# Loading q and k of the first four chunks uncast on SyncE's queue and transposing them in fp32

## The chip, the core and the metric

The kernel runs on one core of one Trainium2 chip. TensorE (PE in the profile; PEld is its weight load) multiplies matrices, VectorE (DVE), ScalarE (ACT) and GpSimd (POOL) work elementwise, SyncE (SP) only issues DMAs. The metric is the device time of one execution in microseconds, the median over runs.

## The reference

The first half is a decaying linear attention with q, k, v of shape (4, 8, 768, 64), that is batch 4, 8 heads, 768 positions, 64 channels; the second half a feed-forward block over the 3072 tokens of 512 channels that come out.

```
for b in range(nb):                       # blocks of 64 positions
    intra = (qb @ kb^T * Dmask) @ vb      # Dmask[i,j] = lam**(i-j) for i >= j, else 0
    inter = (qb * lam**(pos+1)) @ kv_state
    out[block] = intra + inter
    kv_state = lam**64 * kv_state + (kb * lam**(63-pos))^T @ vb
x = out as (batch*positions, heads*channels)
h = x @ w_in                              # 512 -> 2048
g = where(h > 0, h, exp(min(h, 0)) - 1)
return g @ w_out                          # 2048 -> 512, fp32
```

All inputs and the output are fp32. The kernel multiplies in fp16 and sums in fp32.

## The kernel before

The kernel uses blocks of 128 positions. A chunk is one block of one batch with all 8 heads, 128 x 512; there are 24, numbered so that chunks 0 to 3 are the first blocks of the four batches. Chunks 0 to 3 are handled one at a time, later ones in pairs. Each chunk goes through these steps, and the letters are those of the order strings:

- loads of q, k and v. GpSimd issues them (`emit_load`, L109); its DMAs cast fp32 to fp16 on the way. Only q0 comes another way: it is loaded as fp32 on SyncE's queue (L117) and cast by VectorE (L127).
- T: q and k are transposed, 4 + 4 transposes of 128 x 128 (L283). VectorE scales q on the way out of PSUM (L290), ScalarE copies k (L291). From chunk 8 on, DMA transposes on SyncE's queue do this (L268).
- S: scores, 8 matmuls in pairs (L302); VectorE multiplies them by the mask (`pp`, L318).
- P: `pp` times v (L338), plus the state times q from chunk 4 on (L344); ScalarE or VectorE evacuates the result as `xt`, the input of the feed-forward part.
- d, U, M: GpSimd scales k (`kd`, L174), TensorE multiplies it with v (L397, L406), VectorE adds it to the state (L416, L418), GpSimd decays the old state first (`stt`, L378). z and Z set the two copies of a batch's state to zero.
- `1:g:j`: a quarter of the first feed-forward matmul of chunk g, 16 matmuls into `psH` (L478). It uses pieces 2j and 2j+1 of w_in (`i0` to `i7`). ScalarE makes exp and relu of it (L484, L485), VectorE combines them to `g` (L457). `psH` has two buffers.
- `2:g:j`: a quarter of the second, 4 matmuls of 512 columns into `psM` (L499), with pieces 2j and 2j+1 of w_out (`o0` to `o7`).
- `wN`: N dummy matmuls on zeros (L84); ten more stand at the start.

The order is written out by hand: `OPEN` is TensorE's order of steps from the start up to about chunk 8, after which a rule goes on. Each engine works through its instructions in that order and waits in place. `POOL_ORDER` is GpSimd's own order: loads of chunks (k0, q1, ...), weight pieces (i, o), kd (d) and state decays (m). At most eight of GpSimd's DMAs are under way: the ninth issue waits for the landing of the first. `FIRST` orders the preparation: `c0` is the table of scales qs (ScalarE), `c1` the mask (VectorE), `c2` the scales for kd. `BANKS` gives each step its PSUM banks.

The deferred work of VectorE and ScalarE on results (pp, xt, state updates) goes into a list `late`, of which each `1:` and `2:` step takes one entry; a U step empties it.

Of the kernel before, what the change touches and what calls it, by code (L numbers as in the profile page):

```python
# [662 lines left out]
```

## Time and profile before

| | us |
|---|---|
| median of 3 runs | 216.19 (215.58 to 216.25) |
| the profiled execution, whole | 215.0 |
| its span | 213.2 |
| TensorE busy | 202.7 |
| VectorE busy | 130.1 |
| ScalarE busy | 129.0 |
| GpSimd busy, DMA issues included | 96.2 |
| GpSimd's DMA queue | 79760 packets, 13.50 MB written |
| SyncE's DMA queue | 22192 packets, 10.76 MB |

In the lines of the profile a group reads: start, busy time, engine, line of the kernel, operation, output<-inputs, shape and count; in brackets the idle time of that engine just before and what ended it. Times of a group of matmuls include the latency of the last one, so groups overlap: 16 matmuls of 128 columns take 0.89 us of TensorE's time from start to start, 4 of 512 columns 0.86 us. The GB/s of a window are bytes written; a casting load reads twice what it writes.

### The profile page before, as it was taken

The numbers are of one execution on the slowest core, as the hardware profiler recorded it, in microseconds if no ns is written. First come the engines' busy times: TensorE is split into PE (matmuls) and PEld (weight loads), VectorE is DVE, ScalarE is ACT, GpSimd is POOL, SyncE is SP. The second block draws the span as 40 slices with busy tenths as digits, with TensorE's granted clock in tenths as the row PEclk, the third lists the DMA queues.
The fourth block names the chain that finished last, engine by engine and source line by source line (L and its number), as shares of the span: only waits on it lengthen the run. The fifth ranks groups of instructions, "written<-read, shape, count | busy, mean of one in ns | idle before, by whom it ended". The sixth has DMA issues, their size and how long they took to land.

```text
span 213.2 us, 5156 instructions
## 1 busy us (share of the span) xinstructions
PE 202.7 (95%) x2066; PEld 138.1 (65%) x2066; DVE 130.1 (61%) x224; ACT 129.0 (61%) x245; POOL 96.2 (45%) x115
## 2 busy tenths in 40 slices
PE   7667999999999999999999999999999999999994
PEld 2355676767686776766766766766766666666652
DVE  3936453777846888677667667667667547533321
ACT  4545654884867756676476476476476576477640
POOL 7996991999972908667166259300000000000000
PEclk9999999999999999999999999999999999999999
DMA  8999999999996999999939919999124110110112
GB/s 90 141 175 193 192 148 173 147 165 147 153 165 145 111 197 107 144 122 116 129 106 125 167 59 103 144 180 161 52 65 83 52 49 0 54 51 16 36 49 98
DMA packets 101976, 24.59 MB, mean 115 GB/s; under 512 B 92608, under 2 KB 99008, under 8 KB 101952
## 3 DMA queue, kind: packets, MB, share of 16 engines
q0 software_dynamic: 79760, 13.50, 83.1%
q1 hardware_dynamic: 22192, 10.76, 24.6%
q8 instruction: 16, 0.26, 0.5%
q14 instruction: 8, 0.07, 0.1%
HBM read 27.27 MB, written 6.29 MB: 157 GB/s over the span
## 4 chain that ended last, share of the span: by engine, by line
PE 82%; POOL 8%; DMA 7%; issue 1%; ACT 1%; DVE 0%; POOLq 0%; ACTq 0%
PE psM L499 36%; PE psH L478 35%; DMA wi<-in_moe_w_in_dram 4%; DMA wo<-in_moe_w_out_dram 3%; PE psO L338 3%; PE psS L302 3%; PE psO L344 2%; POOL kd L174 1%; POOL wi L148 1%; POOL kn L109 1%; POOL vn L109 1%; PE psU L406 1%; PE psT L283 1%; POOL qn L109 1%; POOL wo L155 1%
## 5 line engine op out<-in xcount | busy, mean ns | idle before, releaser
L478 PE MATMUL psH<-xt,wi 128*128 128x256 f16 (+1 forms) x896 | 99.3, 258 | 2.0 <-DMA wi<-in_moe_w_in_dram 1.1
L457 DVE SCALAR_TENSOR_TENSOR g<-e,psH 128x512 f16<-128x512 f32 x96 | 65.8, 686 | 56.7 <-ACT psH L485 56.0
L484 ACT ACTIVATE e<-psH 128x512 f32<-128x512 f32 x96 | 57.3, 597 | 65.0 <-PE psH L478 62.8
L499 PE MATMUL psM<-wo,g 128*128 128x512 f16 (+1 forms) x384 | 95.6, 377 | 0.7 <-DMA wo<-in_moe_w_out_dram 0.7
L478 PEld LDWEIGHTS <-wi 128*128 128x128 f16 x896 | 76.9, 98 | 27.4 <-DMA wi<-in_moe_w_in_dram 1.8
L485 ACT ACTIVATE psH<-psH 128x512 f32<-128x512 f32 x96 | 57.0, 593 | 0.0
L499 PEld LDWEIGHTS <-g 128*128 128x128 f16 x384 | 35.9, 98 | 29.3 <-issue 1.3
L318 DVE TENSOR_TENSOR pp<-psS,mask 128x512 f16<-128x512 f32 x48 | 30.8, 684 | 4.4 <-PE psS L302 4.4
L174 POOL TENSOR_TENSOR kd<-kn,ks 128x512 f16<-128x512 f16 x20 | 20.7, 1040 | 21.3 <-DMA kn<-in_k_dram 20.4
L378 POOL TENSOR_TENSOR stt<-st,upp 64x256 f32<-64x256 f16 x32 | 19.5, 608 | 14.7 <-DVE st L418 8.9
L109 POOL DMA_DIRECT2D vn<-in_v_dram x14 | 15.5, 1108 | 1.7 <-DMA wi<-in_moe_w_in_dram 1.7
L109 POOL DMA_DIRECT2D kn<-in_k_dram x14 | 15.5, 1105 | 0.8 <-POOLq L647 0.8
L525 ACT COPY osb<-psM 128x512 f32<-128x512 f32 x23 | 13.5, 590 | 3.2 <-PE psM L499 3.2
L109 POOL DMA_DIRECT2D qn<-in_q_dram x13 | 14.8, 1138 | 0.0
L418 DVE TENSOR_TENSOR st<-stt,psU 64x256 f16<-64x256 f32 x32 | 13.3, 416 | 1.2 <-PE psU L406 0.5
L361 DVE TENSOR_TENSOR xt<-psO,qs 128x512 f16<-128x512 f32 x16 | 11.0, 688 | 3.5 <-PE psO L344 3.5
L338 PE MATMUL psO<-pp,vn 128*64 128x128 f16 x192 | 12.0, 222 | 1.2 <-DMA vn<-in_v_dram 1.0
L338 PEld LDWEIGHTS <-vn 128*64 128x64 f16 x192 | 9.7, 110 | 4.6 <-issue 2.9
L344 PE MATMUL psO<-qT,st 128*64 128x128 f16 x160 | 10.0, 219 | 0.0
L344 PEld LDWEIGHTS <-st 128*64 128x64 f16 x160 | 8.9, 110 | 0.0
L302 PE MATMUL psS<-qT,kT 64*128 64x128 f16 x192 | 7.9, 218 | 0.3 <-ACT kT L291 0.3
L359 ACT CAST xt<-psO 128x512 f16<-128x512 f32 x8 | 4.4, 588 | 6.4 <-PE psO L338 4.3
(44 smaller groups left out, 72.3 us busy)
## 6 DMA issues: line engine op xcount, KB each, us to landing
out_dram<-osb SPq DMA_DIRECT2D x23, 256.0 KB, 2.2
kn<-in_k_dram POOLq DMA_DIRECT2D x10, 256.0 KB, 7.8
qn<-in_q_dram POOLq DMA_DIRECT2D x10, 256.0 KB, 6.8
vn<-in_v_dram POOLq DMA_DIRECT2D x10, 256.0 KB, 7.6
wi<-in_moe_w_in_dram POOLq DMA_DIRECT2D x8, 256.0 KB, 6.9
wo<-in_moe_w_out_dram POOLq DMA_DIRECT2D x8, 256.0 KB, 7.7
kn<-in_k_dram POOLq DMA_DIRECT2D x4, 128.0 KB, 4.2
vn<-in_v_dram POOLq DMA_DIRECT2D x4, 128.0 KB, 5.5
```

The lines of the kernel that those rows point to most:

```text
L109: nc.gpsimd.dma_start(out=t[:].rearrange("p b h d -> p (b h) d"), in_=src)
L174: nc.gpsimd.tensor_tensor(out=kd[:], in0=of(kg, g), in1=ks[:].unsqueeze(2).broadcast_to([128, H, 64]), op=ALU.mult,)
L302: nc.tensor.matmul(psS[g][hh][:, hp, :], lhsT=kt[r, hp, :], rhs=qt[r, hp, :], start=True, stop=True,)
L318: nc.vector.tensor_tensor(out=P[:], in0=pts[hh][:], in1=mask[:, hh::2, :], op=ALU.mult)
L338: nc.tensor.matmul(po[r, hp, :], lhsT=vt[:, 2 * hp + hh, :], rhs=Pt[(g, hh)][:, hp, :], start=True, stop=(cb == 0), skip_group_check=True,)
L344: nc.tensor.matmul(po[r, hp, :], lhsT=st[b][cb % 2][:, hp, r], rhs=qt[:, hp, :], start=False, stop=True, skip_group_check=True,)
L378: nc.gpsimd.tensor_tensor(out=tmp[r], in0=old[r, :, r], in1=upp[r].unsqueeze(2).broadcast_to([64, NHP, 64]), op=ALU.mult,)
L457: nc.vector.scalar_tensor_tensor(out=g[:].rearrange("p f c t -> p (f c t)"), in0=e[:], scalar=-1.0, in1=r[:], op0=ALU.add, op1=ALU.min,)
L478: nc.tensor.matmul(pH[:, f * n * 128 : (f + 1) * n * 128], lhsT=wi16[i][:, kk, w * 128 : (w + 1) * 128], rhs=xg[g0][:, kk, :], start=(kk = ...
L484: nc.scalar.activation(e[:], pH[:], AF.Exp)
L485: nc.scalar.activation(pH[:], pH[:], AF.Relu)
L499: nc.tensor.matmul(psM[g][:, cols], lhsT=gts[(g, j * FB + f)], rhs=wo16[i][:, w, cols], start=first and f == 0, stop=end and f == FB - 1, ...
```

## The change

q and k of chunks 0 to 3 are loaded as fp32 on SyncE's queue (`load_raw`). The fp32 tiles of q have two buffers, so q0, k0, q1, k1 are issued at once and q2, k2 after T0, q3, k3 after T1. T0 to T3 transpose the fp32 tiles with an fp32 identity into fp32 PSUM tiles (T3 gets a second bank); kd of these chunks reads the fp32 k. The cast of q0 is gone. GpSimd's order begins with the iota, then loads only v and weights until chunk 4. The mask is made in two halves. The zeroing of the state covers only the parts off the diagonal, in two instructions for each copy. `OPEN` up to the step `B:P4:P5:U4:U5` is in a new order; U no longer empties the list `late`, and a token `f` takes one entry of it.

```diff
--- before.py
+++ after.py
@@ -45,25 +45,27 @@
     WI = [2] * 8
     WO = [2] * 8
     POOL_ORDER = (
-        "k0 k1 iota q1 k2 v1 i0 v0 q2 i1 v2 i2 o0 i3 d0 q3 o1 i4 k3 i5 o2 o3 v3 d1 m4 d2 d3 i7 "
-        "o4 o5 i6 o7 k4 o6 q4 m5 k6 v4 q6 k10 q10 d5 d4 d6 m6 v6 k8 q8 v8 d7 m7 v10"
+        "iota v0 v1 i0 i1 v2 i2 i3 o0 o1 d0 i4 i5 o2 o3 d1 v3 d2 i7 o4 o5 i6 m4 o7 k4 o6 q4  "
+        "m5 d3 k6 v4 q6 k10 q10 d5 d4 d6 m6 v6 k8 q8 v8 d7 m7 v10"
     )
-    RAW = "q0"
-    FIRST = "q0:0 c0 c1 c2"
+    RAWBUFS = 2
+    RAW = "q0 k0 q1 k1 q2 k2 q3 k3"
+    FIRST = "c0 c2"
     OPEN = (
-        "z1 z0 z3 Z1 Z2 Z0 z2 T0 w2 T1 S0 S1 w6 P0 P1 T2 1:0:0 S2 1:1:0 P2 U0 M 1:2:0 1:0:1 2:0:0 "
-        "1:1:1 2:1:0 1:2:1 T3 2:2:0 1:0:2 S3 1:2:2 2:2:1 2:1:1 P3 1:1:2 1:3:0 2:0:1 2:0:2 "
-        "2:1:2 1:1:3 U1 1:2:3 M Z3 2:2:2 1:3:2 U2 1:3:1 2:1:3 1:0:3 T5 T4 2:2:3 1:3:3 S4:5 "
-        "2:0:3 2:3:2 2:3:0 M U3 M B:P4:P5:U4:U5 W8 2:3:3 1:4:1 T6 W9 1:4:0 T7 2:3:1 1:4:3 S6:7 "
-        "1:4:2 2:4:0 2:5:0 1:4:5 1:4:4 2:4:1 B:P6:P7:U6:U7 1:4:7 1:6:1 2:5:2 2:5:1 1:6:0 1:4:6 "
-        "2:4:2 S8:9 1:6:2 1:6:3 2:4:3 2:5:3 W11 W10 1:6:4 B:P8:P9:U8:U9 1:6:5 1:6:6 2:6:0 "
-        "2:6:1 L12 1:6:7 2:6:2 1:8:0 S10:11 2:6:3 1:8:1 2:7:0 1:8:2 2:7:1"
+        "c1 c3 Z1 Z2 Z0 T0 w1 T1 S0 S1 w3 P0 P1 z0 z1 z2 z3 w2 1:0:0 T2 1:1:0 S2 U0 1:0:1 U1 P2  "
+        "1:1:1 M f 1:2:0 f 2:0:0 f 1:2:1 2:1:0 T3 1:0:2 S3 2:2:0 1:1:2 M P3 1:2:2 2:0:1 2:1:1  "
+        "1:3:0 U2 2:2:1 2:0:2 M 1:3:1 2:1:2 1:0:3 1:1:3 Z3 2:2:2 1:2:3 1:3:2 2:1:3 T5 T4  "
+        "2:2:3 1:3:3 S4:5 2:0:3 2:3:2 2:3:0 U3 M f f f f B:P4:P5:U4:U5 W8 2:3:3 1:4:1 T6 W9  "
+        "1:4:0 T7 2:3:1 1:4:3 S6:7 1:4:2 2:4:0 2:5:0 1:4:5 1:4:4 2:4:1 B:P6:P7:U6:U7 1:4:7  "
+        "1:6:1 2:5:2 2:5:1 1:6:0 1:4:6 2:4:2 S8:9 1:6:2 1:6:3 2:4:3 2:5:3 W11 W10 1:6:4  "
+        "B:P8:P9:U8:U9 1:6:5 1:6:6 2:6:0 2:6:1 L12 1:6:7 2:6:2 1:8:0 S10:11 2:6:3 1:8:1 2:7:0  "
+        "1:8:2 2:7:1"
     )
...
     BANKS = (
         "S0=M0,M1 S1=C,D S2=D,M1 S3=D,B P0=M1 P1=B P2=B P3=D U0=M0 U1=D U2=A U3=M1 T0=M1,C "
-        "T1=D,A T2=A,D T3=D T4=M0 T5=A T6=M1 T7=D M2=C M3=M0"
+        "T1=D,A T2=A,D T3=D,C T4=M0 T5=A T6=M1 T7=D M2=C M3=M0"
     )
...
@@ -109,24 +111,16 @@
         nc.gpsimd.dma_start(out=t[:].rearrange("p b h d -> p (b h) d"), in_=src)
 
 
-    raw = {}
-    for w in RAW.split():
-        x = {"q": q, "k": k}[w[0]]
-        g0 = int(w[1:])
-        raw[w] = asb.tile([128, H, 64], FP32, name=f"raw_{w}", tag=f"raw_{w}")
-        (nc.sync if w[0] == "q" else nc.scalar).dma_start(
-            out=raw[w][:], in_=x[g0, :, 0:L].rearrange("h p d -> p h d")
-        )
+    def load_raw(w):
+        x, g0 = {"q": q, "k": k}[w[0]], int(w[1:])
+        t = asb.tile([128, 1, H, 64], FP32, name=f"raw_{w}", tag=f"raw_{w[0]}", bufs=RAWBUFS if w[0] == "q" else 4)
+        (qg if w[0] == "q" else kg)[g0] = t
+        nc.sync.dma_start(out=t[:, 0], in_=x[g0, :, 0:L].rearrange("h p d -> p h d"))
+
+    raws = RAW.split()
+    for w in raws[: 2 * RAWBUFS]:
+        load_raw(w)
     nc.scalar.preload_act_table_set("natural_log_exp_and_others")
-
-    def cast_raw(g, w, eng):
-        n = f"{w}{g}"
-        t = asb.tile([128, 1, H, 64], FP16, tag=f"{w}n1", name=f"{w}n{g}", bufs=4)
-        (qg if w == "q" else kg)[g] = t
-        if eng == 0:
-            nc.vector.tensor_copy(t[:, 0], raw[n][:])
-        else:
-            nc.scalar.copy(t[:, 0], raw[n][:])
 
     def of(tiles, g):
         g0, i = group_of[g]
@@ -190,14 +184,24 @@
 
     def emit_pool_run():
         while pool_list and pool_list[0][0] != "m":
+            if pool_list[0][0] == "d" and group_of[int(pool_list[0][1:])][0] not in kg:
+                break
             emit_pool()
 
     assert "iota" in POOL_ORDER.split("d0")[0]
     while pool_list and pool_list[0][0] not in "dm":
         emit_pool()
 
+    def zero_off(b, i, eng):
+        for hh in range(2):
+            part = st[b][i][hh * 64 : (hh + 1) * 64, :, (1 - hh) * 64 : (2 - hh) * 64]
+            if eng is nc.vector:
+                eng.memset(part, 0.0)
+            else:
+                eng.memzero(part)
+
     def zero_st1(b):
-        nc.vector.memset(st[b][1][:], 0.0)
+        zero_off(b, 1, nc.vector)
 
 
     loglam = cpool.tile([128, H], FP32, name="loglam")
@@ -205,6 +209,7 @@
     pos = cpool.tile([128, 3], FP32, name="pos")
     row = cpool.tile([128, 128], FP32, name="row")
     ident16 = cpool.tile([128, 128], FP16, name="ident16")
+    ident32 = cpool.tile([128, 128], FP32, name="ident32")
     causT = cpool.tile([128, 128], FP32, name="causT")
     loglam_p = cpool.tile([128, NHP], FP32, name="loglam_p")
 
@@ -218,7 +223,7 @@
     nc.vector.tensor_scalar_mul(pos[:, 1:2], iota_c[:], -1.0)
     nc.scalar.activation(dn[:], loglam[:], AF.Exp, scale=pos[:, 1:2])
     nc.vector.tensor_scalar(
-        out=ident16[:], in0=row[:], scalar1=pos[:, 0:1], scalar2=None, op0=ALU.is_equal
+        out=ident32[:], in0=row[:], scalar1=pos[:, 0:1], scalar2=None, op0=ALU.is_equal
     )
     nc.vector.tensor_scalar(
         out=causT[:], in0=row[:], scalar1=pos[:, 0:1], scalar2=None, op0=ALU.is_ge
...
@@ -234,11 +240,11 @@
                 qs[:, hp, :], row[:], AF.Exp, scale=loglam_p[:, hp : hp + 1]
             )
 
-    def emit_mask():
+    def emit_mask(hh):
         nc.vector.tensor_tensor(
-            out=mask[:],
-            in0=causT[:].unsqueeze(1).broadcast_to([128, H, 128]),
-            in1=dn[:].unsqueeze(2).broadcast_to([128, H, 128]),
+            out=mask[:, hh::2],
+            in0=causT[:].unsqueeze(1).broadcast_to([128, NHP, 128]),
+            in1=dn[:, hh::2].unsqueeze(2).broadcast_to([128, NHP, 128]),
             op=ALU.mult,
         )
 
@@ -273,16 +279,21 @@
 
     def att_T_pe(g):
         n = len(TAGS[f"T{g}"].split())
+        dt, ident = (FP32, ident32) if g < B else (FP16, ident16)
         pts = [
-            bank(f"T{g}", i, [128, 2 // n, NHP, 128], FP16, f"psT{g}_{i}")
+            bank(f"T{g}", i, [128, 2 // n, NHP, 128], dt, f"psT{g}_{i}")
             for i in range(n)
         ]
         pts = [pts[0][:, 0], pts[n - 1][:, 2 // n - 1]]
         for src, pt in zip((of(qg, g), of(kg, g)), pts):
             for hp in range(NHP):
                 nc.tensor.transpose(
-                    pt[:, hp, :], in_=src[:, 2 * hp : 2 * hp + 2, :], identity=ident16[:]
+                    pt[:, hp, :], in_=src[:, 2 * hp : 2 * hp + 2, :], identity=ident[:]
                 )
+        if raws[2 * RAWBUFS + 2 * g :]:
+            for w in raws[2 * RAWBUFS + 2 * g :][:2]:
+                load_raw(w)
+            emit_pool_run()
         qt, kt = [
             asb.tile([128, NHP, 128], FP16, tag=f"{w}T", name=f"{w}T{g}", bufs=6)
             for w in "qk"
@@ -528,7 +539,7 @@
             emit_stores()
 
     def zero_st(b):
-        nc.scalar.memzero(st[b][0][:])
+        zero_off(b, 0, nc.scalar)
 
     def load_pair(g):
         for w in "qkv":
...
@@ -574,12 +584,10 @@
             burst(t)
         elif w == "U":
             late.extend(att_U(*a))
-            while late:
-                late.pop(0)()
         else:
             {"T": att_T_pe, "1": mm1, "2": mm2, "Z": zero_st, "z": zero_st1,
-             "q": lambda g, e: cast_raw(g, "q", e), "k": lambda g, e: cast_raw(g, "k", e),
-             "c": lambda i: (emit_qs, emit_mask, emit_ks)[i](), "W": pool_work, "L": load_pair,
+             "c": lambda i: (emit_qs, lambda: emit_mask(0), emit_ks, lambda: emit_mask(1))[i](),
+             "f": lambda: late and late.pop(0)(), "W": pool_work, "L": load_pair,
              "M": next_M, "w": zero_matmuls}[w](*a)
 
     for t in FIRST.split():
```

More of the change, by code (lines that the diff above doesn't have):

```diff
@@ L228 @@
         nc.vector.tensor_copy(loglam_p[r, :], loglam[r, hh::2])
+    nc.vector.tensor_copy(ident16[:], ident32[:])
     nc.vector.tensor_scalar_add(pos[:, 2:3], pos[:, 1:2], float(L))
@@ L549, in ready @@
             assert g < B or f"U{g - B}" in seen
-        if t[0] == "U" and g < 2 * B:
-            assert f"{'z' if g < B else 'Z'}{g % B}" in seen
+            assert not B <= g < 3 * B or f"{'z' if g < 2 * B else 'Z'}{g % B}" in seen
         if t[0] == "U" and g >= B:
```

## The prediction

> **What bounds the kernel now.** I read the page first, then the busy time by stage, then TensorE's own order of time with what ended each wait, then the chain that ended last, and last the DMA traffic in short windows.
>
> ```profile
> PE 202.7 (95%) x2066; PEld 138.1 (65%) x2066; DVE 130.1 (61%) x224; ACT 129.0 (61%) x245; POOL 96.2 (45%) x115
> ...
> DMA  8999999999996999999939919999124110110112
> ```
>
> TensorE (PE) has something to do for 95% of the span, and the DMA engines are full over the first quarter. The stages, cut at TensorE's waits for data (columns: window, its length, busy us of PE, PEld, DVE, ACT and POOL, granted clock, DMA share, GB/s written):
>
> ```profile
> 5.58:12.90 7.32, 4.44 (x56) 2.44 (x56) 5.78 (x11) 3.12 (x10) 7.25 (x10) 1.00 1.87 148
> 12.90:20.46 7.56, 5.56 (x84) 4.46 (x85) 4.34 (x8) 5.03 (x10) 6.14 (x8) 1.00 1.60 189
> 20.46:34.26 13.80, 13.09 (x154) 9.20 (x155) 6.79 (x11) 8.69 (x16) 11.84 (x14) 1.00 1.37 173
> 34.26:48.90 14.64, 14.64 (x171) 10.10 (x170) 9.77 (x17) 9.50 (x18) 11.25 (x13) 1.00 1.91 159
> ```
>
> TensorE has gaps until 20.46 us; from 20.46 to 34.26 it misses only 0.71 of 13.80, and after that nothing to speak of. So the time is set by when TensorE gets its data up to 20.46 and by how much work is left then. TensorE's order there:
>
> ```profile
> 12.07 0.64 PE L338 MATMUL psO<-pp,vn 128*64 128x128 f16 x16 [1.03 <-DMA vn<-in_v_dram]
> 12.92 0.40 PE L283 MATMUL psT<-ident,qn 128*128 128x128 f16 x4 [0.21 <-DMA qn<-in_q_dram]
> ...
> 14.38 0.62 PE L478 MATMUL psH<-xt,wi 128*128 128x128 f16 x8 [0.40 <-DMA wi<-in_moe_w_in_dram]
> ...
> 18.02 1.79 PE L478 MATMUL psH<-xt,wi 128*128 128x128 f16 x24 [0.60 <-ACT xt L359]
> 20.46 0.62 PE L478 MATMUL psH<-xt,wi 128*128 128x128 f16 x8 [0.66 <-DMA wi<-in_moe_w_in_dram]
> ...
> 21.88 0.59 PE L499 MATMUL psM<-wo,g 128*128 128x512 f16 x2 [0.36 <-DMA wo<-in_moe_w_out_dram]
> ...
> 34.26 1.46 PE L499 MATMUL psM<-wo,g 128*128 128x512 f16 x6 [0.35 <-DMA wo<-in_moe_w_out_dram]
> ```
>
> Nearly every wait ends on a load. The one at 20.46 is w_in piece 3 (i3), the second half of step 1:0:1, and the chain that ended last goes through it:
>
> ```profile
> 11.63 8.79 DMA wi<-in_moe_w_in_dram
> ```
>
> Issued at 11.63, it lands at 20.42: it stands 8.8 us in the queue. The opening is bound by DMA throughput, not by the issue. Short windows show what a loaded DMA system moves:
>
> ```profile
> 3.10:3.50 0.40, 0.40 (x2) 0.15 (x1) 0.00 (x0) 0.00 (x0) 0.33 (x4) 1.00 1.16 247
> 3.55:3.95 0.40, 0.40 (x2) 0.15 (x1) 0.35 (x4) 0.21 (x1) 0.40 (x2) 1.00 1.52 228
> 4.20:5.20 1.00, 0.99 (x4) 0.22 (x2) 0.95 (x6) 0.56 (x3) 1.00 (x2) 1.00 2.26 144
> 12.00:20.00 8.00, 6.20 (x100) 4.93 (x100) 4.11 (x7) 5.21 (x10) 6.97 (x9) 1.00 1.62 187
> ```
>
> In the first, SyncE's (SP's) uncast load of q0 runs alone: 247 GB/s written, and as much read. In the third, GpSimd's (POOL's) casting loads of k run alone: 144 written, which is 288 read, since fp32 becomes fp16. In the fourth mostly weights: 187 written, 374 read. A q or k chunk (262,144 B) thus costs the DMA engines 1.06 us on SP's queue and 0.91 us on POOL's; a weight piece (524,288 B) 1.40 us. The second window has both queues at work and 228 written, which is 82% of the first rate and 18% of the third: the queues share one capacity, and SP's gets most of it.
>
> **Part by part.** The profiled execution took 215.0 us, its span 213.2 and 1.8 around it; the median of the runs is 216.19, 1.19 above it. I sum a difference and put it on the median.
>
> *Loads.* Seven POOL loads (k0 to k3, q1 to q3) become SP loads. POOL loses seven issues of some 0.9 us, 6.4 us, which hide today behind the 8.8 us queue. SP gains seven issues of 0.41 us; lam stays ahead of them and SP's next entry, the first store, comes after 40 us, so nothing waits behind them. q2 waits on SP until T0 has read q0's buffer and q3 until T1 has read q1's; k2 and k3 stand behind these. The price is on the shared engines: 7 x (1.06 - 0.91) = +1.05 us in total.
>
> When does i3 land? Before, ahead of it stood q0, eight POOL chunks and i0, i1, i2, o0. Changed, ahead of it on POOL are only v0, v1, v2, i0, i1, i2, but SP's eight chunks get the larger share, so they are through before it. From 3.1 us on (0.4 us of q0 done): before, 0.66 + 8 x 0.91 + 5 x 1.40 = 14.9, that is 18.0, against 20.42 measured: 2.4 of lag. Of this I put 0.7 to stretches in which POOL's issue held the engines back (128 GB/s at 5.60 to 8.00 and 154 at 8.00 to 12.00, against 144 to 187). Changed: 8.08 + 3 x 0.91 + 4 x 1.40 = 16.4, that is 19.5, with a lag between 0 (nothing behind i3 is served early) and 1.7: 19.5 to 21.2. If q3 and k3 are not through, up to 2.1 less. I take 20.1, the middle of 19.1 and 21.2: -0.3 us against 20.42.
>
> *Order.* When TensorE meets the wait for i3 today it has done step 1:2:0 and P2; in the new order both come after 1:0:1. That is 16 matmuls (0.89 us, as 16 take in the chain) and 8 of P (about 0.23): +1.1 us still to do when i3 comes. Everything ahead of it has slack: k1 lands near 8.4 (q0 at 4.5 as now, three more at 1.3 each), T1 and S0 follow at 8.9, P1 some 3 us later as now (four pp of 0.62), 1:0:0 at 12.6, and T2, 1:1:0, S2, U0 end at 15.8, even if i1 is late by 2 us. That slack of 2 to 4 us before 20.1 covers the dropped cast (0.67 on DVE), the two mask halves, the smaller zeroings (eight of ScalarE's and eight of VectorE's instead of four each, under 0.3 us apiece), the dummy matmuls and U's deferred updates; if i3 came before 15.8, S0's wait behind T1 would be late next.
>
> After i3 the new order has 1:0:1, U1, P2, 1:1:1, 1:2:0 in a row. ACT needs 0.60 + 0.59 for each 1: step and 0.59 for P2's xt, so 1:2:0 stands about 0.65 behind ACT and the psH that DVE frees. Against it, the waits for w_out at 21.88 and 34.26 (0.36 + 0.35) should go: o1 comes 2.8 us after i3 and is wanted after 3.6; w_out piece 5 comes after nine weight pieces and a chunk, 13.5, and is wanted after 15. Sum -0.05. For U1, kd1 stands on POOL behind o3, whose issue waits for v2 (near 17.4); 0.75 + 1.04 later is 19.2, before 20.5.
>
> *fp32 transposes.* T0 to T3, 32 of them; T0 to T2 lie in the slack, T3's eight on the path. No fp32 transpose is in the trace. Lower end: as fp16, eight in 0.45 us, 56 ns each, no extra. Upper end: the 512-column slot, 216 ns, 160 extra, +1.3 us for T3. The changed program has no separate weight load beside them, and a load takes 98 ns; I take twice the slot, 56 extra: +0.45 us. VectorE's and ScalarE's evacuations (0.68 and 0.58) read 512 elements as before: nothing, or at most the 0.1 by which a 512-element fp32 copy (0.59) differs.
>
> Sum: -0.3 + 1.1 - 0.05 + 0.45 = +1.2 us; 216.19 + 1.2 = 217.4.
>
> **A rule against it.** The Trainium skill, DMA: Bandwidth & Descriptors, Rules for kernel authors, says that spreading DMAs over SP, ACT and GpSimd gains no bandwidth, as all run on the same 16 engines, and saves issue time alone. By that rule i3 comes no earlier and the sum stays; the window 3.55 to 3.95 agrees (228 GB/s, between 247 and 144).
>
> **Rivals.** 1, faster: the two queues add up when weights are in flight, and small chunks ride at the 374 GB/s read of the weights stage. Then 11 chunks cost 0.70 each: 3.1 + 7.3 + 5.6 = 16.0, with 1.7 of lag 17.7, and the sum is -2.7 + 1.1 - 0.05 + 0.45 = -1.2, 215.0. For it: weights do reach 374. Against it: the mixed window. It decides when i3 lands before 19.2. If SP's loads cost nothing at all, TensorE would run from 12.6 to 13.2 on, some -2: 214.2.
>
> 2, no change: q3 and k3 fall behind i3, which lands near 19.2, and the order's 1.1 and T3's 0.45 eat it: 216.2.
>
> 3, clearly slower: the clock drops in the long wait before i3. The dummy matmuls at the start come every 0.43 us, six later ones take 1.47:
>
> ```profile
> 3.72 0.15 PEld L84 LDWEIGHTS <-zero 128*128 128x128 f16 x1 [0.27 <-issue]
> ...
> 4.15 0.15 PEld L84 LDWEIGHTS <-zero 128*128 128x128 f16 x1 [0.28 <-issue]
> ...
> 9.57 1.47 PE L84 MATMUL psZ<-zero 128*128 128x512 f16 x6
> ```
>
> So there is a half speed, left after 3.4 us of work (1.19 to about 4.6). If it returns before i3, 3.4 us of full work lose 1.7: 217.4 + 1.7 = 219.1. T3 at its upper end gives 218.2. For it: six dummies are left in the opening instead of eight, and T0 and T1 wait for loads one after the other. Against it: today's gap from 10.9 to 12.07 does no harm. The Trainium skill, TensorE: Matmul & The Clock Gate, PE-mode transpose, says that transposes do not count as busy for the clock; no run here shows it.
>
> **How the numbers follow.** Forecast 0.45, rival 1 0.28, rival 2 0.14, rival 3 0.13. Two runs of this kernel are told apart from about 0.3%, 0.65 us. Slower 0.58, same 0.14, faster 0.28. The forecast's own range is 216.9 to 218.5 (i3 at 19.5 or 21.2); with the rivals, 214.4 to 219.4.
>
> **What would show it.** Right: i3's wait ends between 19.5 and 21, SP's eight chunks have landed by 16, TensorE reaches the wait with 1:2:0 undone, then no wait for w_out; a transpose of T3 every 100 ns or so. Wrong: TensorE without gaps from 18 us or before (rival 1); GB/s written with both queues busy well over 230; T2 or T3 waiting for q or k on SP's queue, which would mean that POOL's queue gets the larger share.

## The result, and the profile after

The changed kernel takes 222.37 us (median; 222.06 to 223.73). The kernel before, run beside it, took 216.22 (215.58 to 216.27). The ratio is 1.030, with a 95% interval of 1.026 to 1.035. The forecast was 217.4, with a range of 214.4 to 219.4: the direction is right, the size is not, and the time lies above the range. The medians differ by 6.15 us. In the profiled executions, one of each kernel, the span grew from 213.2 to 220.3 us, by 7.1.

All of it is lost in the opening. `B:P4:P5:U4:U5` is the first step that has the same place in both orders with the same work behind it. Its first matmul, from TensorE's order of time in the kernel before (start, busy us, engine, line, operation, shape, count):

```profile
48.90 0.25 PE L338 MATMUL psO<-pp,vn 128*64 128x128 f16 x2
```

and in the kernel after:

```profile
55.94 0.25 PE L349 MATMUL psO<-pp,vn 128*64 128x128 f16 x2
```

It starts 7.04 us later, and what remains from there is 164.3 us (213.2 - 48.90) before and 164.4 (220.3 - 55.94) after. So the start of this step, called the mark below, measures the opening. The page of the kernel after, its busy times and the granted clock in 40 slices of 5.5 us:

```profile
PE 205.5 (93%) x2064; PEld 140.9 (64%) x2064; DVE 129.7 (59%) x229; ACT 130.4 (59%) x249; POOL 90.3 (41%) x108
...
PEclk9958999999999999999999999999999999999999
```

TensorE is busy longer, for nearly the same work: the fp32 transposes take longer, and in the third slice and in part of the fourth it is granted half the clock. Its order of time up to the mark has these waits (in brackets the idle time before, and what ended it):

```profile
10.47 0.65 PE L290 MATMUL psT<-ident,raw_q 128*128 128x128 f32 x4 [3.61 <-DMA raw_q<-in_q_dram]
13.78 1.12 PE L290 MATMUL psT<-ident,raw_k 128*128 128x128 f32 x4 [2.65 <-DMA raw_k<-in_k_dram]
...
19.72 0.61 PE L290 MATMUL psT<-ident,raw_q 128*128 128x128 f32 x4
22.67 0.66 PE L290 MATMUL psT<-ident,raw_k 128*128 128x128 f32 x4 [2.34 <-DMA raw_k<-in_k_dram]
...
26.52 2.22 PE L489 MATMUL psH<-xt,wi 128*128 128x128 f16 x32 [0.18 <-DVE g L468]
...
44.36 1.05 PE L489 MATMUL psH<-xt,wi 128*128 128x128 f16 x16 [0.20 <-DVE g L468]
...
47.37 1.05 PE L489 MATMUL psH<-xt,wi 128*128 128x128 f16 x16 [0.20 <-DVE g L468]
...
50.17 0.38 PE L290 MATMUL psT<-ident,qn 128*128 128x128 f16 x4 [0.44 <-ACT osb L536]
```

The waits for w_in piece 3 and for w_out are gone. In their place TensorE waits for q1, k1 and k2, all on SyncE's queue (and 0.40 us for k0); T2 has its q at 19.72 and stands until k2 is there at 22.6. Everything behind T2 on TensorE stands too, also 1:0:1, whose second weight piece (w_in piece 3) has landed at 19.43. The chain that ended last goes through the same loads (start, length, what):

```profile
1.66 4.28 DMA raw_k<-in_k_dram
...
7.32 15.31 DMA raw_k<-in_k_dram
...
22.67 0.66 PE psT L290 x4
...
31.45 1.07 PE psT L290 x8
```

k2 is issued at 7.32 and lands 15.31 us later. The DMA issues of the page (median us from issue to landing in the last column) show that GpSimd's weights also land later, 11.7 and 12.6 us against 6.9 and 7.7 before:

```profile
wi<-in_moe_w_in_dram POOLq DMA_DIRECT2D x8, 256.0 KB, 11.7
wo<-in_moe_w_out_dram POOLq DMA_DIRECT2D x8, 256.0 KB, 12.6
...
raw_q<-in_q_dram SPq DMA_DIRECT2D x4, 256.0 KB, 9.8
raw_k<-in_k_dram SPq DMA_DIRECT2D x4, 256.0 KB, 12.7
```

How the two queues share is seen in the records of single packets. Counted in five windows of the kernel after (a packet on SyncE's queue carries 256 B; on GpSimd's 128 B written for v, 512 B for w_in, 1024 B for w_out, each read as twice that; in the third, fourth and fifth column packets, in the last two GB/s read):

```
window us     GpSimd loads   SyncE   GpSimd                   SyncE  GpSimd
4.0 to 4.5    just starting    499   17 of 128 B                255       9
12.5 to 13.0  v                200   209 of 128 B               102     107
16.5 to 17.0  w_in             121   121 of 512 B                62     248
19.0 to 21.0  w_out            311   298 of 1024 B, 8 of 512     40     309
23.0 to 25.0  w_in             488   466 of 512 B, 2 of 1024     62     241
```

In the last four windows the two queues send one packet each, whatever the packets carry, and so they do over the long run: from 9.0 to 29.5 us SyncE's queue sends 4,839 and GpSimd's 4,773. Four bytes of w_in, or eight of w_out, are read for each byte of q or k. A chunk of q or k has 1024 packets. At 121 in 0.5 us it takes 4.2 us beside w_in, at 311 in 2 us 6.6 beside w_out, at 200 in 0.5 us 2.6 beside v; the forecast had 1.06. So, counted through, the data packets of k1 end at 12.6 us, of k2 at 20.8, of q3 at 25.5 and of k3 at 31.5. A load lands somewhat later than that: SyncE's queue sends sixteen packets of 4 B for each load, of which k2's last, counted the same way, goes at 22.2, and k2 lands at 22.63. Only in the first window does SyncE's queue have the engines nearly to itself, and it moves at the rate of a chunk in 1.0 us.

The equal turns don't hold everywhere. From 5.2 to 6.2 us SyncE's queue sends 49 packets and GpSimd's 1,030, although the issue of q1 has ended at 3.58 and that of k1 at 4.58; from 7.0 to 8.0 it is 554 and 269. So q1 is late for another reason too, and what holds SyncE's queue in that stretch stays open.

The Trainium skill, DMA: Bandwidth & Descriptors, Queues, rings and completion order, says that each DMA engine goes round robin between the queue rows that have work, a packet at a time. The equal counts above agree; the stretch from 5.2 to 6.2 us would only if SyncE's queue had nothing ready then, which the records don't tell. The page counts several descriptors to a packet, and whether a record of the trace is such a packet or one descriptor no run here shows. The prediction weighed another rule of that page and not this one.

### The profile page after: what moved, and what is told of

It is laid out like the page before. It is cut to its first block, busy times and chain, and to the rows that moved or that the text cites. A ratio compares the mean times of both kernels' runs of the same rounds, so it can differ in the third digit from the quotient of the medians.

```text
span 220.3 us, 5168 instructions
## 1 busy us (share of the span) xinstructions
PE 205.5 (93%) x2064; PEld 140.9 (64%) x2064; DVE 129.7 (59%) x229; ACT 130.4 (59%) x249; POOL 90.3 (41%) x108
## 4 chain that ended last, share of the span: by engine, by line
PE 84%; DMA 9%; ACT 3%; DVE 1%; SPq 1%; issue 0%; ACTq 0%
PE psH L489 37%; PE psM L510 36%; DMA raw_k<-in_k_dram 9%; PE psS L313 3%; PE psO L349 3%; PE psO L355 2%; PE psT L290 2%; ACT e L495 1%; DVE g L468 1%; ACT psH L496 1%; PE psU L417 1%; SPq L118 0%; PE psMrest L522 0%; ACT osb L536 0%; PE psU L408 0%
## 5 line engine op out<-in xcount | busy, mean ns | idle before, releaser
L389 POOL TENSOR_TENSOR stt<-st,upp 64x256 f32<-64x256 f16 x32 | 19.5, 608 | 18.3 <-DVE st L429 13.2
L168 POOL TENSOR_TENSOR kd<-kn,ks 128x512 f16<-128x512 f16 x16 | 16.7, 1047 | 23.0 <-DMA kn<-in_k_dram 22.3
L536 ACT COPY osb<-psM 128x512 f32<-128x512 f32 x23 | 13.5, 591 | 3.1 <-PE psM L510 3.1
L111 POOL DMA_DIRECT2D qn<-in_q_dram x10 | 11.9, 1190 | 0.5 <-DMA vn<-in_v_dram 0.5
L111 POOL DMA_DIRECT2D kn<-in_k_dram x10 | 11.6, 1164 | 0.3 <-DMA wo<-in_moe_w_out_dram 0.3
L301 DVE TENSOR_TENSOR qT<-psT,qs 128x512 f16<-128x512 f32 (+1 forms) x8 | 5.4, 685 | 5.9 <-PE psT L290 5.9
## 6 DMA issues: line engine op xcount, KB each, us to landing
wi<-in_moe_w_in_dram POOLq DMA_DIRECT2D x8, 256.0 KB, 11.7
wo<-in_moe_w_out_dram POOLq DMA_DIRECT2D x8, 256.0 KB, 12.6
raw_k<-in_k_dram SPq DMA_DIRECT2D x4, 256.0 KB, 12.7
```

The costliest lines, as they stand in the source:

```text
L111: nc.gpsimd.dma_start(out=t[:].rearrange("p b h d -> p (b h) d"), in_=src)
L168: nc.gpsimd.tensor_tensor(out=kd[:], in0=of(kg, g), in1=ks[:].unsqueeze(2).broadcast_to([128, H, 64]), op=ALU.mult,)
L389: nc.gpsimd.tensor_tensor(out=tmp[r], in0=old[r, :, r], in1=upp[r].unsqueeze(2).broadcast_to([64, NHP, 64]), op=ALU.mult,)
```

## The experiments

The letters are those of the recorded expectations, and A is the theory that the late loads on SyncE's queue hold TensorE. Ratios are to the kernel before, run beside each. The table gives the start of the mark and, last, its lateness against the 48.90 of the kernel before. The mark belongs to one profiled execution, the ratio to several runs of each kernel, and the two can differ by over 1 us: e1's profiled execution was the fastest of its four, so its ratio stands for 4.4 us where its mark has 2.97.

| kernel | ratio (95%) | mark us | late us |
|---|---|---|---|
| changed kernel | 1.030 (1.026 to 1.035) | 55.94 | 7.04 |
| e1 new order alone | 1.020 (1.014 to 1.027) | 51.87 | 2.97 |
| e2 new loads alone | 1.048 (1.042 to 1.054) | 59.42 | 10.52 |
| e3 weights held back | 1.016 (1.011 to 1.022) | 52.21 | 3.31 |
| e4 more dummies | 1.041 (1.034 to 1.049) | 56.20 | 7.30 |
| e5 k0, k1 on ScalarE's queue | 1.026 (1.022 to 1.030) | 54.60 | 5.70 |
| e6 only two chunks uncast | 1.010 (1.007 to 1.013) | 51.62 | 2.72 |
| e7 before, later weights first | 0.998 (0.996 to 1.000) | 48.78 | -0.12 |
| e8 e7, i3 ahead of o0 | 1.000 (0.997 to 1.003) | 47.84 | -1.06 |
| e9 e1 with kd1 earlier | 1.013 (1.009 to 1.018) | 51.23 | 2.33 |
| e10 w_in in smaller packets | 1.034 (1.030 to 1.038) | 55.47 | 6.57 |
| e11 T2 later | 1.044 (1.039 to 1.048) | 58.39 | 9.49 |
| e12 T2 later, U1 behind it | 1.033 (1.030 to 1.036) | 56.53 | 7.63 |

### The order and the loads apart

e1 has the new order, the mask in halves and the smaller zeroings, but the loads and the fp16 transposes of before:

```diff
--- before.py
+++ e1
-    FIRST = "q0:0 c0 c1 c2"
+    FIRST = "q0:0 c0 c2"
     OPEN = (
-        "z1 z0 z3 Z1 Z2 Z0 z2 T0 w2 T1 S0 S1 w6 P0 P1 T2 1:0:0 S2 1:1:0 P2 U0 M 1:2:0 1:0:1 2:0:0 "
...
+        "c1 c3 Z1 Z2 Z0 T0 w1 T1 S0 S1 w3 P0 P1 z0 z1 z2 z3 w2 1:0:0 T2 1:1:0 S2 U0 1:0:1 U1 P2  "
...
```

> The new order of the opening with the loads of before (q0 uncast on SyncE's queue and cast on VectorE, all else on GpSimd, fp16 transposes). Theory A (the loss is SyncE's queue: its packets take turns one by one with GpSimd's larger ones, so k2 lands at 22.6 us instead of about 12.5): i3 lands near 20.4 us as before, T2 waits for nothing long, and what is left is the order: 1.1 us more work behind i3, and steps 1:g:j that stand behind ScalarE and VectorE, 0.5 to 2 us; 217.3 to 219.3 us in all. Rival B (the order is the main loss): 220.5 us or more. Rival C (the order costs nothing): 215.8 to 216.8.

e2 has the new loads and fp32 transposes in the order of before:

```diff
--- before.py
+++ e2
     POOL_ORDER = (
-        "k0 k1 iota q1 k2 v1 i0 v0 q2 i1 v2 i2 o0 i3 d0 q3 o1 i4 k3 i5 o2 o3 v3 d1 m4 d2 d3 i7 "
...
+        "iota v0 v1 i0 i1 v2 i2 i3 o0 o1 d0 i4 i5 o2 o3 d1 v3 d2 i7 o4 o5 i6 m4 o7 k4 o6 q4  "
...
-    RAW = "q0"
-    FIRST = "q0:0 c0 c1 c2"
+    RAWBUFS = 2
+    RAW = "q0 k0 q1 k1 q2 k2 q3 k3"
+    FIRST = "c0 c1 c2"
```

> The order of before with the new loads, GpSimd's new order and the fp32 transposes. Theory A: k2 lands near 22.6 us again, and since this order has T2 ahead of the first step 1:0:0, TensorE stands still until then; 222 to 225 us. Rival B (the order is the main loss): under 218.5. T's eight transposes take 1.07 us as in the changed kernel, against 0.45.

e1 took 219.04 us and e2 225.36, beside 214.83 of the kernel before. By its time e1 lies in what A gave and e2 0.4 above; by their ratios both cost more than A gave, as the kernel before was faster beside them than in its first runs. TensorE's waits in e1:

```profile
12.49 0.64 PE L352 MATMUL psO<-pp,vn 128*64 128x128 f16 x16 [2.04 <-DMA vn<-in_v_dram]
...
19.70 0.62 PE L492 MATMUL psH<-xt,wi 128*128 128x128 f16 x8 [0.64 <-DMA wi<-in_moe_w_in_dram]
...
21.95 0.40 PE L411 MATMUL psU<-vn,kd 128*128 128x128 f16 x4 [1.63 <-POOL kd L175]
...
46.10 0.39 PE L297 MATMUL psT<-ident,qn 128*128 128x128 f16 x4 [0.44 <-ACT osb L539]
```

and in e2:

```profile
22.91 0.73 PE L281 MATMUL psT<-ident,raw_k 128*128 128x128 f32 x4 [2.47 <-DMA raw_k<-in_k_dram]
23.43 1.91 PE L480 MATMUL psH<-xt,wi 128*128 128x128 f16 x16
```

e2 waits for k2 as the changed kernel does, but T2 stands ahead of 1:0:0 there, so even the first feed-forward matmul begins at 23.43, at half clock (1.91 for sixteen instead of 1.06). The two parts cost 2.97 and 10.52 us by the mark, and together 7.04, not 13.5: the new order has more work ahead of T2, which would soften the loads. Without the loads it is a loss of its own, which the forecast had at 1.1. The wait of U1 for kd1 is not in the changed kernel; in e1 kd1 stands late in GpSimd's order. T4's 0.44 for `osb` is in both.

e9 takes that wait out of e1:

```diff
--- e1
+++ e9
-        "k0 k1 iota q1 k2 v1 i0 v0 q2 i1 v2 i2 o0 i3 d0 q3 o1 i4 k3 i5 o2 o3 v3 d1 m4 d2 d3 i7 "
+        "k0 k1 iota q1 k2 v1 i0 v0 q2 i1 v2 i2 o0 i3 d0 d1 q3 o1 i4 k3 i5 o2 o3 v3 m4 d2 d3 i7 "
```

> The new order alone again, with kd1 moved up on GpSimd to stand right behind kd0. Theory A (the order costs TensorE time through what its moved steps wait for, and U1's wait for kd1, 1.63 us, is one of those waits): that wait goes, most of it is gained, ratio to the kernel before 1.010 to 1.016 against 1.0203 of the order alone. Rival B (U1's wait only fills time that would be lost to w_in piece 3 or to the 1: steps in any case): the ratio stays at 1.018 to 1.022, and another wait of over 1 us stands within 3 us of U1's place.

It took 217.67, ratio 1.013, inside what A gave; but its interval and that of e1 overlap, and the mark moved by only 0.64 us. TensorE's order shows why so little:

```profile
20.73 0.62 PE L492 MATMUL psH<-xt,wi 128*128 128x128 f16 x8 [1.81 <-DMA wi<-in_moe_w_in_dram]
21.19 0.39 PE L411 MATMUL psU<-vn,kd 128*128 128x128 f16 x4
```

U1 follows without a wait, and the wait for w_in piece 3 has grown from 0.64 to 1.81, which is a sign of rival B. It isn't kd1's doing on GpSimd, where this piece stands ahead of kd0 and kd1: its issue starts at 11.62 in e1 and at 11.63 in e9, but it lands at 19.66 and at 20.68. Why it landed a microsecond later isn't shown; in the kernel before it landed at 20.42. So how much of the order's cost was U1's wait stays unsettled.

### Is it SyncE's queue, or its neighbour?

In e3 kd0 and kd1 stand ahead of the weights on GpSimd, so no weight is issued before k1 has landed:

```diff
--- after.py
+++ e3
-        "iota v0 v1 i0 i1 v2 i2 i3 o0 o1 d0 i4 i5 o2 o3 d1 v3 d2 i7 o4 o5 i6 m4 o7 k4 o6 q4  "
+        "iota v0 v1 d0 d1 i0 i1 v2 i2 i3 o0 o1 i4 i5 o2 o3 v3 d2 i7 o4 o5 i6 m4 o7 k4 o6 q4  "
```

> The changed kernel with kd0 and kd1 moved ahead of the first weights in GpSimd's order: kd1 waits for k1, so that no weights are under way while q0, k0, q1, k1 load. Theory A (turns packet by packet): k1 lands between 8 and 10 us instead of 13.8, since only v0 and v1 share the engines with it; k2 lands near 17 to 18; the whole 216.5 to 219 us. Rival D (SyncE's queue is slow in itself, whatever GpSimd has under way: its issues take 1.3 to 3.3 us): k1 still lands after 12.5 us, k2 near 22, and the weights come later, so 222 us or more.

Its issues, with the time to landing, and its TensorE waits:

```profile
raw_q<-in_q_dram SPq DMA_DIRECT2D x4, 256.0 KB, 5.0
raw_k<-in_k_dram SPq DMA_DIRECT2D x4, 256.0 KB, 5.0
```

```profile
9.27 0.66 PE L290 MATMUL psT<-ident,raw_q 128*128 128x128 f32 x4 [1.51 <-DMA raw_q<-in_q_dram]
10.46 0.97 PE L290 MATMUL psT<-ident,raw_k 128*128 128x128 f32 x4 [0.53 <-DMA raw_k<-in_k_dram]
...
16.27 0.62 PE L489 MATMUL psH<-xt,wi 128*128 128x128 f16 x8 [0.81 <-DMA wi<-in_moe_w_in_dram]
...
18.18 0.62 PE L489 MATMUL psH<-xt,wi 128*128 128x128 f16 x8 [1.29 <-DMA wi<-in_moe_w_in_dram]
18.63 0.61 PE L290 MATMUL psT<-ident,raw_q 128*128 128x128 f32 x4
19.08 0.60 PE L290 MATMUL psT<-ident,raw_k 128*128 128x128 f32 x4
```

With no neighbour the same loads on the same queue take 1.2 us each (1,714 packets from 10 to 12 us) and land 5.0 us after issue instead of 9.8 and 12.7. All eight have landed by 15.0 and T2 does not wait. The queue itself is not slow, and rival D falls. k1 lands at 10.41, a little later than A gave, and k2 at 12.80, well before A's 17 to 18. 3.7 of the 7.0 us come back by the mark, and by the ratios 1.4% of 3.0%. Of the rest, part is that 1:0:0 now waits for the weights that were held back: these loads were traded against each other.

e10 changes only the neighbour's packets: w_in comes in 16 pieces of 128 columns, 256 B written to a packet.

```diff
--- after.py
+++ e10
-    WI = [2] * 8
+    WI = [1] * 16
-        "iota v0 v1 i0 i1 v2 i2 i3 o0 o1 d0 i4 i5 o2 o3 d1 v3 d2 i7 o4 o5 i6 m4 o7 k4 o6 q4  "
+        "iota v0 v1 i0 i1 i2 i3 v2 i4 i5 i6 i7 o0 o1 d0 i8 i9 i10 i11 o2 o3 d1 v3 d2 i14 i15 o4 o5 i12 i13 m4 o7 k4 o6 q4  "
```

> The changed kernel with w_in in 16 pieces of 128 columns instead of 8 of 256, so that GpSimd's packets are 256 B on the writing side instead of 512. Theory A (SyncE's and GpSimd's queues take turns packet by packet, so a q or k chunk beside w_in waits for as many of GpSimd's packets as it has itself, whatever their size): beside w_in a chunk takes 2.6 to 3.3 us instead of 4.2, k2 lands at 16 to 20 instead of 22.6, T2 starts by 20.2, w_in piece by piece comes later, and the time is 217 to 221.5. Rival G (the queues share by bytes, and the size of the packets is nothing): k2 lands within 0.8 us of 22.6 and the time within 0.5% of the changed kernel's 222.4 or above it, since the extra issues cost GpSimd 0.9 us each.

From 18 to 19 us SyncE's queue moved 333 packets and GpSimd's 332 of 256 B: again one each, now 3.1 us a chunk instead of 4.2. k2 lands at 18.34 instead of 22.63, and T2 starts without a wait. Sharing by bytes (rival G) falls. But the time is 222.34, no better, and there A missed. TensorE's order in e10:

```profile
19.49 0.60 PE L290 MATMUL psT<-ident,raw_k 128*128 128x128 f32 x4
...
24.29 0.40 PE L408 MATMUL psU<-vn,kd 128*128 128x128 f16 x4 [1.68 <-POOL kd L168]
...
24.96 3.52 PE L489 MATMUL psH<-xt,wi 128*128 128x128 f16 x32
```

and its busy times by window, of 24.9 to 28.3 us (length, busy us of PE, PEld, DVE, ACT and POOL, granted clock, DMA share, GB/s):

```profile
24.90:28.30 3.40, 3.40 (x39) 3.34 (x34) 0.73 (x3) 1.67 (x3) 2.59 (x4) 0.53 1.67 180
```

GpSimd has twice as many w_in issues, the later of which wait for earlier ones to land, and reaches kd1 only at 23.18, so U1 waits 1.68 us; and the 32 matmuls behind it run at a granted clock of 0.53. In the chain they take 3.46 us, against 1.78 for two groups of 0.89 in the kernel after: another 1.7. These two took back nearly all that the earlier k2 gave: the mark comes only 0.47 earlier.

### Other ways to bring the loads in

e6 takes q and k of chunks 2 and 3 back to GpSimd, cast, q2 and k2 ahead of the weights:

```diff
--- after.py
+++ e6
-        "iota v0 v1 i0 i1 v2 i2 i3 o0 o1 d0 i4 i5 o2 o3 d1 v3 d2 i7 o4 o5 i6 m4 o7 k4 o6 q4  "
+        "iota v0 v1 q2 k2 i0 i1 v2 i2 i3 o0 d0 q3 o1 i4 k3 i5 o2 o3 d1 v3 d2 i7 o4 o5 i6 m4 o7 k4 o6 q4  "
-    RAW = "q0 k0 q1 k1 q2 k2 q3 k3"
+    RAW = "q0 k0 q1 k1"
-        dt, ident = (FP32, ident32) if g < B else (FP16, ident16)
+        dt, ident = (FP32, ident32) if g < 2 else (FP16, ident16)
```

> The changed kernel with q and k of chunks 2 and 3 back on GpSimd (cast, fp16 transposes), q2 and k2 ahead of the first weights. Theory A: SyncE's four loads now take turns with small packets only; k1 lands near 11, T2 waits for nothing, i3 lands near 18 to 19, and the wait that cost most is gone; what stays is the order, with TensorE less far behind: 1.000 to 1.013 times before. Rival B (most of the loss is the order): 1.018 or more, as with the order alone (1.020).

217.22 us beside 214.95, ratio 1.010, as expected. T2 starts at 18.18 without a wait, and the mark comes 4.3 us earlier than in the changed kernel. In TensorE's order:

```profile
12.30 1.11 PE L290 MATMUL psT<-ident,raw_k 128*128 128x128 f32 x4 [1.67 <-DMA raw_k<-in_k_dram]
...
18.18 0.39 PE L290 MATMUL psT<-ident,qn 128*128 128x128 f16 x4
```

What is left, 2.72, is close to e1's 2.97, but it isn't the order alone: T1 still waits for k1 on SyncE's queue, until 12.30, and the granted clock is half from 8.74 to 15.56 us, with no load to wait for behind it that would hide this.

e5 loads k0 and k1 on ScalarE's queue:

```diff
--- after.py
+++ e5
-        nc.sync.dma_start(out=t[:, 0], in_=x[g0, :, 0:L].rearrange("h p d -> p h d"))
+        (nc.scalar if w in ("k0", "k1") else nc.sync).dma_start(out=t[:, 0], in_=x[g0, :, 0:L].rearrange("h p d -> p h d"))
```

> The changed kernel with k0 and k1 issued from ScalarE's queue; q0 to q3, k2 and k3 stay on SyncE's. Theory A (every queue with work gets one packet in turn): with three queues the two fp32 ones get two packets of three, so k1 lands between 8 and 10.5 us instead of 13.8, k2 between 16 and 19 instead of 22.6; 1.005 to 1.02 times before. Rival F (GpSimd's queue gets half of the turns, however many others there are): k1 not before 12.5, k2 near 22; 1.025 to 1.035.

220.8 us, ratio 1.026, which lies in F's range and not in A's. k1 is there at 9.80 without a wait, as A has it and F has not, but q0 now comes later (T0 at 7.19 instead of 4.99), and k2 misses A's 16 to 19:

```profile
20.05 1.12 PE L290 MATMUL psT<-ident,raw_k 128*128 128x128 f32 x4 [3.93 <-DMA raw_k<-in_k_dram]
```

The half clock comes late here, from 19.88 to 23.30 us, and T2's k transposes and the work behind them run under it. From 8.7 to 11.7 us the records show 2 packets on SyncE's and ScalarE's queues and 1,916 of GpSimd's loads, though q2's and k2's issues end at 8.2 and 8.9. Taking turns doesn't explain that stretch, and like the one from 5.2 to 6.2 us in the changed kernel it stays open.

### The clock

e4 puts 17 dummy matmuls between T0 and T1 instead of 1:

```diff
--- after.py
+++ e4
-        "c1 c3 Z1 Z2 Z0 T0 w1 T1 S0 S1 w3 P0 P1 z0 z1 z2 z3 w2 1:0:0 T2 1:1:0 S2 U0 1:0:1 U1 P2  "
+        "c1 c3 Z1 Z2 Z0 T0 w17 T1 S0 S1 w3 P0 P1 z0 z1 z2 z3 w2 1:0:0 T2 1:1:0 S2 U0 1:0:1 U1 P2  "
```

> The changed kernel with 17 dummy matmuls instead of 1 between T0 and T1, which fill TensorE from 6.5 to about 10.4 us, while it waits for q1 anyway. The granted clock should stay whole beyond 11.3 us, where it falls to half now until 18.0. Theory A: T1 to P1 get quicker by about 1 us, but T2 still waits for k2 until 22.6, so the end stays: 222.0 to 222.7. Rival E (the half clock costs the 1.7 us of the prediction's third rival): 220.3 to 221.3.

The dummies moved the half clock but didn't prevent it, from some 11.35 to 18.2 us in the kernel after to these windows (columns as above):

```profile
10.00:13.50 3.50, 1.20 (x8) 0.65 (x6) 0.69 (x1) 0.00 (x0) 1.50 (x3) 1.00 1.46 171
13.50:20.35 6.85, 6.46 (x51) 3.84 (x52) 3.77 (x12) 1.66 (x3) 3.13 (x4) 0.50 1.35 184
```

T2's k comes at 22.59 and the mark at 56.20, as late as ever; the median, 223.02 us, lies above what either theory gave. So the run doesn't price the clock; it shows that with k2 at 22.6 a half clock ahead of T2 is hidden in this execution. Where it falls behind T2 it is not: in e2 it is half from 23.30 to 26.71 us and in e5 from 19.88 to 23.30, with TensorE at work nearly all of the time, which I estimate at some 1.7 us each, half of 3.41. In the profiled executions the kernel before has no half clock in its opening after 4.61 us, and all versions with the new order or the new loads have 3.4 us of it or more. e7, in the old order, has it too, from 13.39 to 16.80, and its mark is no later. What of the loss the clock makes up in the executions that were not profiled isn't known.

### Working around the late k2

e11 puts 1:1:0, U0, U1 and 1:0:1, which need nothing of chunk 2, ahead of T2:

```diff
--- after.py
+++ e11
-        "... w2 1:0:0 T2 1:1:0 S2 U0 1:0:1 U1 P2  "
-        "1:1:1 M f 1:2:0 f 2:0:0 f 1:2:1 2:1:0 T3 ..."
+        "... w2 1:0:0 1:1:0 U0 U1 f f 1:0:1 T2  "
+        "1:1:1 S2 2:0:0 M P2 f 1:2:0 f f 1:2:1 2:1:0 T3 ..."
```

> The changed kernel with the steps 1:1:0, U0, U1 and 1:0:1, which need nothing of chunk 2, put ahead of T2; all loads as in the changed kernel, so k2 lands at the same 22.6 us. Theory A (TensorE works in order, and the 2.34 us at T2 are lost only because work that has its data is queued behind the waiting transposes): T2 starts at 22.3 to 23.5 with less than 0.4 us of wait ahead of it, step B:P4 starts 1.5 to 2.4 us earlier than its 55.94, and the time falls by 1.5 to 2.4 us, ratio to the kernel before 1.019 to 1.026 against 1.030. Rival H (three 1: steps ahead of T2 only trade this wait for one on w_in piece 3, on kd1 or on ScalarE and VectorE): step B:P4 starts within 0.6 us of 55.94, the ratio stays at 1.028 to 1.033, and waits of 1.5 us and more stand between 19.7 us and T2.

Ratio 1.044, slower still: A missed, and the mark lies beyond H's range too. T2's k transposes wait 2.04 us and start at 25.90. k2 had landed by 23.54, where GpSimd's kd2 starts on it. The profile names no cause of the wait, but by `BANKS` the transposes need PSUM bank D, which held U1's result until VectorE had copied it out at 25.80. That wait is of the edit's own making, so e12 puts U1 behind S2:

```diff
--- e11
+++ e12
-        "... w2 1:0:0 1:1:0 U0 U1 f f 1:0:1 T2  "
-        "1:1:1 S2 2:0:0 M P2 f 1:2:0 f f 1:2:1 2:1:0 T3 ..."
+        "... w2 1:0:0 1:1:0 U0 1:0:1 f T2  "
+        "1:1:1 S2 U1 2:0:0 2:1:0 M P2 f f 1:2:0 f f 1:2:1 T3 ..."
```

> As the run before, but U1, whose PSUM bank T2's k transposes need, stands behind S2 instead of ahead of T2, and 2:0:0 and 2:1:0 lie between S2 and P2. Theory A (the wait at T2 is a blocked queue): nothing waits for the bank; T2's k transposes start at 23.3 to 24 with 1:1:0 and 1:0:1 done; these are 1.8 us of TensorE work, less the 0.6 to 1.3 us that T2 starts later than its 22.67, so step B:P4 starts 0.5 to 1.2 us ahead of its 55.94, ratio 1.023 to 1.030. Rival H (the wait is only traded for others): step B:P4 starts at 55.7 or later, ratio 1.030 or more, with waits of 1 us or more for ScalarE, VectorE or GpSimd between 19 and 34 us.

222.27 us, ratio 1.033, and the mark at 56.53: rival H is right, though no single wait reaches its 1 us. T2 doesn't wait any more, and others do:

```profile
22.49 1.05 PE L489 MATMUL psH<-xt,wi 128*128 128x128 f16 x16 [0.78 <-DVE g L468]
...
23.82 0.60 PE L290 MATMUL psT<-ident,raw_k 128*128 128x128 f32 x4
...
26.43 0.38 PE L408 MATMUL psU<-vn,kd 128*128 128x128 f16 x4 [0.78 <-DVE pp L329]
27.02 1.89 PE L510 MATMUL psM<-wo,g 128*128 128x512 f16 x8 [0.21 <-DVE pp L329]
...
29.93 1.95 PE L489 MATMUL psH<-xt,wi 128*128 128x128 f16 x32 [0.68 <-ACT xt L370]
```

0.78 + 0.78 + 0.21 + 0.68 = 2.45 us of waits stand where 2.34 + 0.18 stood. My reading is that with the `1:` steps used up ahead of T2 little is left to cover chunk 2's way through T, S, `pp`, P and `xt`. The wait at T2 was the place at which a late chunk showed, and moving the place gained nothing; of the versions tried, only those that bring the loads in earlier gained (e3 and e6, and e5 a little), and e10 shows that even this can be lost again.

### Is there something to gain in the kernel before?

e7 lets GpSimd issue the later weight pieces ahead of the decay m4 and of kd2 and kd3; e8 also brings i3 ahead of o0, and 1:1:1 ahead of 2:0:0.

```diff
--- before.py
+++ e7
-        "... o2 o3 v3 d1 m4 d2 d3 i7 o4 o5 i6 o7 ..."
+        "... o2 o3 v3 d1 i7 o4 o5 i6 m4 d2 d3 o7 ..."
```

> The kernel before with four weight pieces (i7, o4, o5, i6) issued ahead of m4, kd2 and kd3 on GpSimd. From 26 to 34 us the DMA engines move 158 GB/s instead of 187 to 193, because these issues come late. The wait of 0.35 us for w_out piece 5 at 34.26 should go: 0.3 to 0.6 us less than before (0.997 to 0.9985). A rival is that kd2 and the state decay come late then and a U step waits: same or up to 0.5 us more.

```diff
--- e7
+++ e8
-        "... i2 o0 i3 d0 q3 ..."
+        "... i2 i3 o0 d0 q3 ..."
-        "... 1:2:0 1:0:1 2:0:0 1:1:1 2:1:0 ..."
+        "... 1:2:0 1:0:1 1:1:1 2:0:0 2:1:0 ..."
```

> As e7, and in addition w_in piece 3 ahead of w_out piece 0 on GpSimd, and step 1:1:1 ahead of 2:0:0 on TensorE. i3 should land 1.4 us sooner, near 19.0, and TensorE, which reaches it at 19.8, should not wait for it (0.66 us) nor for w_out piece 1 (0.36): 0.5 to 1.3 us less than before (0.994 to 0.998). A rival: three 1: steps in a row wait for ScalarE (0.60 + 0.59 each against 0.89 of TensorE): 0.3 less or the same.

214.74 and 214.71 us beside 214.95: neither can be told from no change. e7's ratio, 0.998, lies in its forecast, e8's, 1.000, does not. In e8 piece 3 lands at 17.84 and nothing waits for it, but TensorE waits 0.72 us for `g` at 20.95, a wait of the kind that its rival names. Its profiled execution reached the mark 1.06 us earlier, and it was the fastest of its ten. No version tried clearly beats the kernel before.

## Why the prediction was wrong

The step that failed is the sharing of the DMA engines: "the queues share one capacity, and SP's gets most of it", so that "SP's eight chunks get the larger share, so they are through before" w_in piece 3. It rested on the window 3.55 to 3.95 us of the kernel before. By packets this window holds 283 of q0 on SyncE's queue and 145 of GpSimd's first loads, two for one, that is 73% of the first rate of the prediction and 32% of the third, not 82 and 18. But GpSimd's queue is only starting there: it sends 6 packets from 3.2 to 3.3 us, 33 from 3.6 to 3.7 and 56 from 3.9 to 4.0, where SyncE's also sends 56; q0 ends at 4.1. So the window shows a start, and the forecast took it for the lasting share. From 9 to 29.5 us in the kernel after the shares are equal in packets, a fifth of the bytes for q and k beside w_in, a ninth beside w_out. The sentence that named what would make the forecast wrong, T2 waiting on SyncE's queue because GpSimd's gets the larger share, is what happened. The forecast's sum also asked only when w_in piece 3 lands: its rival 2 had q3 and k3 fall behind this piece, as they and k2 did, and gave the wait for them no price.

From that step the rest follows. "That slack of 2 to 4 us" had k1 near 8.4 and T2, 1:1:0, S2 and U0 done at 15.8; k1 landed at 13.73, and T2 started its k at 22.67. So the term for the loads was -0.3 and measured some 2 to 4: at the mark the changed kernel is 4.07 us later than e1 and 4.32 later than e6, but by the ratios it is 1.0% slower than e1, some 2.2 us, and 2.0% slower than e6, some 4.4. These differences hold the fp32 transposes too.

The other terms:

- *w_in piece 3 at 20.1* was about right (it landed at 19.43, and nothing waited for it), and it no longer decided anything. The 1.05 us of total DMA cost, priced as throughput, was the wrong kind of price: the loads were late by their place in the turns.
- *No wait for w_out, kd1 in time behind U1*: right in the changed kernel (kd1 starts at 16.13, before U1's 25.61).
- *Order +1.1*: too small. e1 shows 2.97 by the mark and 4.4 by the ratio, in part a wait that e1 has and the changed kernel hasn't; e6, with U1 in time, still shows 2.72, in which k1's lateness and the half clock have a share. Of the order's waits the changed kernel shows 0.18 + 0.20 + 0.20 before `1:` steps that follow one another closely, and 0.44 at T4: 1.02 us. The forecast had given "1:2:0 stands about 0.65 behind ACT" and set it off against the w_out waits; it looked no further than 1:2:0.
- *fp32 transposes +0.45*: eight take 1.07 us in the chain, 134 ns each, against 0.45 in fp16. +0.62, within its bounds.
- *Rival 3, the half clock*: the mechanism came (half clock from some 11.35 to 18.2 us), but in the profiled execution it is covered by the wait for k2. e10 shows the price where it isn't: 1.7 us, the size that the rival had.
- *The ranges*: with piece 3 at 19.5 the forecast's own sum gives 216.8, not 216.9, and the ends 214.4 and 219.4 of the whole range are not worked out; the rivals give 214.2 and 219.1.

Rival 1 (the queues add up) is refuted by the rates read, summed from the table of packets: 209 GB/s with v, 310 with w_in, 349 with w_out, while the stage of mostly weights in the kernel before reached 374 and SyncE's queue alone 255. This agrees with the rule that the prediction weighed (the Trainium skill, DMA: Bandwidth & Descriptors, Rules for kernel authors: spreading over the queues gains no bandwidth); what it leaves out is which queue then waits.

What is shown and what only argued: that the neighbour's packets make the loads late is shown (e3, e10, the counts). That late loads cost some 2 to 4 us of the 6 to 7 is shown by e1, e3 and e6. That the order costs something of its own is shown by e1; its split over single waits is not, and neither is how much of the rest is the half clock, since no version with the new order was run that keeps the clock whole.

## What to carry to other kernels

In most windows here a second DMA queue beside a busy one got its turn by packets, not by bytes: price a load with small packets by its number of packets times the neighbour's turn, and read a share only from a window in which both queues have had work for some time. Before moving loads, ask for the in-order engine what stands behind the first instruction that uses them, and what covers the chain behind it; putting other work ahead shifted the wait here (e11, e12), and an earlier load took it away (e3, e6). Where two changes come together (loads and order here), run each alone: the costs by the mark, 3.0 and 10.5 us, didn't add to the 7.0 of both.
